# Block sums over two engines, earlier second probabilities and an earlier state load in an attention and feed-forward kernel

## The chip, the cores and the metric

The kernel runs on one core of one Trainium2 chip. The metric is the device time of one execution in microseconds (us), the median of several runs. TensorE is PE, VectorE is DVE, ScalarE is ACT, GpSimd is POOL, and SyncE, whose queue issues most transfers, is SP.

## The reference

There are 8 batches of 8 heads. Each head has 512 rows of x and 32 rows of state, both 64 wide. Rows of x attend to the state and rows of the state attend to x; the 544 rows that come out, all heads side by side, go through a feed-forward layer with a leaky relu.

```python
scores = scale * np.matmul(x, state.transpose(0, 1, 3, 2))
a = softmax(scores)                     # over the 32 rows of state
xread = np.matmul(a, state)
scores2 = scale * np.matmul(state, x.transpose(0, 1, 3, 2))
a2 = softmax(scores2)                   # over the 512 rows of x
sread = np.matmul(a2, x)
t = np.concatenate([xread, sread], axis=2)   # heads side by side: 4352 x 512
h = t @ w_in                                 # 512 x 2048
g = np.maximum(0.01 * h, h)
return g @ w_out                             # 2048 x 512
```

## The kernel before, in words

The kernel works batch by batch. The order of each engine's instructions is the order in which they are recorded in the source (a manual schedule), so an instruction that waits holds all that follow it on its engine.

**The softmax of a batch.** PE makes the scores of the batch (`a_scores`, L256) into the PSUM tile `sc`. DVE takes the maxima of blocks of 32 (`a_max`, L266, tile `mrow`), spreads them (L274) and subtracts (L280, tile `sh`): together `a_shift`. ACT takes the exponential (`a_exp`, L284, tile `e1`). DVE sums, adds a small number (L293), takes the reciprocal (L296), spreads it (L298) and multiplies (`a_probs`, L302): the first probabilities `aT`. For the second softmax, DVE takes maxima along the rows (`a_max2`, L331), ACT makes the exponentials with their sums (`a_exp2`, L337), and `a_probs2` is four DVE instructions: L345, L347 and two at L355. The second probabilities are transposed by a DMA on SP (`a_a2t`, L362; for batches 0 and 1 together `a_a2t_pair`, L369), and `a_sread` (L380) multiplies them with x.

**x and the state.** x of batch 2 and later is loaded in float32 (`load_x`, tile `xl`), cast to bfloat16 (`cast_all` on POOL, L132, tile `xb`) and transposed by a DMA on SP (`a_xt_dma`, L234, tile `xT`). The state of batches 4 to 7 is loaded by eight transfers on SP (`load_state(1)`, L203), cast on POOL (`state_cast`, L209) and transposed on SP (`state_t`, L214).

**Feed-forward.** `ff1` (L428) multiplies 128 columns of M (the state times w_in, `a_m`, copied from PSUM by `m_evict`) with `aT`, and ACT writes the leaky relu (L433) into `hT`: 16 steps a batch. The second product of batches 0 and 1 is made by plain pieces (`piece`, L533) between the steps, copied out by `y_store` (L543). The pieces of batch 0's rows 2 and 3 share one PSUM tile of two banks, `wide`. From batch 2 on, and for half of batch 1's rows, the product is done with 7 block products in place of 8. Its operands are sums of blocks of w_out, tiles `tw` 1 to 4 (`tw_sum`, L572; sum 2 needs sum 1, and sum 4 needs sum 2), and sums of blocks of h (`s_sum`, L593; for the half of batch 1 `two_sum`, L669). Batch 1's half is multiplied in the steps of batch 2 by `two_product` (L685), with additions on DVE at L695.

**Order around the change.** Before batch 1's steps: softmax of batch 1, x of batch 2, the block sums 1 and 2, pieces of batch 0, two copies of y and batch 0's second probabilities. Then batch 1's 16 steps s, with the softmax of batch 2 from s = 3 and the transpose of batch 3's x at s = 7. Then batch 2's 16 steps, with the softmax of batch 3 from s = 1.

**SP's transfers.** The transfers of SP stand in one queue, and their completions go round eight semaphores: a transfer waits for the one eight places before it.

Of the kernel before, what the change touches and what calls it, by code (L numbers as in the profile page):

```python
# [9 lines left out]
P = 128  # L10
# [5 lines left out]
NT = S // P  # L16
# [11 lines left out]
def kernel(  # L28
# [99 lines left out]
            xl[b][:, h0:h1].rearrange("p h (t d) -> p h t d", t=NT),  # L128
        )

    def cast_all(b):
        nc.gpsimd.tensor_copy(  # L132
            xt[b][:].rearrange("p t h d -> p h t d"),
            xl[b][:].rearrange("p h (t d) -> p h t d", t=NT),
        )

    def cast_x0(q, copy):
        v = q % 2
# [190 lines left out]
    def a_max2(a):  # L329
        a.m2 = att.tile([P, 2], FP32, name="mcol", tag="mcol")  # L330
        nc.vector.tensor_reduce(out=a.m2[:], in_=a.sc[:], axis=AX.X, op=ALU.max, negate=True)  # L331
# [231 lines left out]
    def tw_sum(n, j0, j1, eng):  # L563
        u, at = j0 // 4, slice(j0 % 4, j0 % 4 + j1 - j0)
        in0, in1 = {
            1: lambda: (w_block(0, 1, j0, j1), w_block(0, 0, j0, j1)),
            2: lambda: (w_block(1, 1, j0, j1), tw[1][u][:, at]),
            3: lambda: (w_block(1, 1, j0, j1), w_block(0, 1, j0, j1)),
            4: lambda: (w_block(1, 0, j0, j1), tw[2][u][:, at]),
        }[n]()  # L570
        with nc.allow_low_precision(reason="operands of bf16 products"):
            eng.tensor_tensor(out=tw[n][u][:, at], in0=in0, in1=in1, op=ALU.subtract)  # L572
# [440 lines left out]
    tw_open()  # L1013
    for j in (4, 6, 0, 2):
        tw_sum(1, j, j + 2, nc.gpsimd)
    for i in (0, 1):
        piece(0, h0, i, 1)
    open_xb(2)
# [22 lines left out]
            piece(0, h0, i, 3, copy=None, js=range(2 * v, 2 * v + 2))  # L1041
    for j in (0, 4):
        tw_sum(2, j, j + 4, nc.vector)
    for i in (2, 3):
        y_store(0, i, VEC)
    cast_all(3)
    a_probs2(a0)


# [3 lines left out]
    for s in range(16):  # L1053
        ff1(a1, h1, s)
        if s % 2:
            pb, hT, i, jq = fill[s // 2]
            piece(pb, hT, i, jq)
        if s in (1, 15):
            for u in range(2):
                tw_sum(3 if s == 1 else 4, 4 * u, 4 * (u + 1), nc.vector)  # L1060
        if s == 3:
            a_scores(a2)
            m_evict(a2, 0, a_m(a2, 0, "big"), SCA)
            a_shift(a2)
            a_max2(a2)
        elif s == 7:
            a_exp(a2)
            a_open(att_of[3], 3)
            a_xt_dma(att_of[3])
        elif s in (9, 11):  # L1070
            a_exp2(a2, s // 2 - 4)
            if s == 9:
                a_recip(a2)
                a_probs(a2)
            else:
                a_probs2(a2)
        elif s == 13:
            a_probs2(a1)
            a_a2t_pair(0)
            pm = [a_m(a2, 1, "big"), a_m(a2, 2, "sc")]  # L1080
            m_evict(a2, 1, pm[0], VEC)
            m_evict(a2, 2, pm[1], SCA)

    for b in range(2, B):
# [2 lines left out]
        a = att_of[b]  # L1089
        nxt = att_of[b + 1] if b + 1 < B else None  # L1090
        if b == 2:
            q1 = two_open(h1, 2 * P, ("S0", "S1"), "py")
            two_keep(q1, "S2")
            fill = {i: [lambda i=i: piece(1, h1, i, 3)] for i in range(2)}
            for s, n in zip((2, 3, 5, 6, 8, 9, 11), (1, 2, 6, 5, 3, 7, 4)):
                fill[s] = [lambda n=n: two_product(q1, n)]
            fill[11].append(lambda: nc.sync.dma_start(pair_rows(1, 1), q1.y[:]))
        else:
            order = (2, 6, 5, 7, 3, 4)
            fill = {  # L1100
                s: [lambda n=order[s // 2], v=s % 2: product(b - 1, n, v)] for s in range(12)
            }
            for i, n in enumerate(order):
                if n not in (2, 7):
                    fill[2 * i + 1].append(lambda n=n: after(b - 1, n))
# [3 lines left out]
        for s in range(16):  # L1109
            ff1(a, hT, s)  # L1110
            if s == 0:
                if b == 2:
                    load_x(4, nc.sync)
                if b + 2 < B:
                    open_xb(b + 2)
                if b == 7:
                    a_a2t_pair(6)
                elif b != 6:
                    a_a2t(a)
                for n in (1, 2):  # L1120
                    if b > 2:
                        s_sum(b - 1, n, 4, 8, nc.vector)
                    else:
                        two_sum(q1, n, 0, 8, nc.vector)
            elif s == 1:
                if nxt is not None:
                    a_scores(nxt)
                m_evict(a, 3, a_m(a, 3, "big"), SCA)
                if nxt is not None:
                    a_max(nxt)  # L1130
                if b > 2:
                    for j in range(0, HJ, 2):
                        s_sum(b - 1, 4, j, j + 2, nc.gpsimd)
                else:
                    for j in (0, 4):
                        two_sum(q1, 4, j, j + 4, nc.gpsimd)
                if b + 2 < B:
                    cast_all(b + 2)
            elif s == 4:
                if b == 2:  # L1140
                    load_state(1)
                    a_sread(a0)
            elif s == 7:
                if b == 2:
                    a_sread(a1)
            elif s == 13:
                if b < 6:
                    a_sread(a)
            elif s == 8:
                if b == 2:  # L1150
                    state_cast(1, nc.gpsimd)
                    state_t(1)
            elif s == 10:
                if b == 7:
                    a_sread(att_of[6])
            elif s == 12:
                if b == 7:
                    a_sread(a)
                for n in (1, 2):
                    s_sum(b, n, 0, 4, nc.vector)  # L1160
                for j in (0, 4):
                    s_sum(b, 3, j, j + 4, nc.vector)
# [25 lines left out]
            if s == 1:  # L1188
                if b > 2:
                    after(b - 1, 2)  # L1190
                if nxt is not None:
                    a_diff(nxt)
                    if b > 2:
                        a_max2(nxt)
            elif s == 3 and b == 2:
                a_max2(nxt)
                two_sum(q1, 3, 0, 8, nc.vector)
            elif s == (8 if b == 2 else 7):
                if b > 2:
                    after(b - 1, 7)  # L1200
                if nxt is not None:
                    a_probs(nxt)
                    a_probs2(nxt)
            elif s == 10 and nxt is not None:
                pm2 = a_m(nxt, 2, "phpy")
                pm0 = a_m(nxt, 0, "big")
                pm1 = a_m(nxt, 1, "sc")
                for g, copy in enumerate((SCA, VEC)):
                    copy(nxt.M[:, g, 2 * DM:3 * DM], pm2[g][:])
                m_evict(nxt, 0, pm0, VEC)  # L1210
                m_evict(nxt, 1, pm1, SCA)
# [76 lines left out]
```

## Time and profile before

| | us |
|---|---|
| median of 3 runs | 203.69 (203.34 to 203.79) |
| profiled execution | 203.5 |
| its span | 201.7 |
| PE busy | 194.7 (97%) |
| DVE busy | 160.9 (80%) |
| ACT busy | 143.8 (71%) |
| POOL busy | 62.7 (31%) |

The granted clock of TensorE is at full speed in all 40 slices of the span. A row of the timeline has the start in us, the time taken, the engine, the line of the source, the operation, out<-in with shapes, how many equal instructions were merged, and in brackets the idle time before it with what ended it. Instructions that follow each other on one engine overlap by some hundredths.

### The profile page before, as it was taken

How to read it: one execution, taken by the hardware profiler on the slowest of the kernel's cores; microseconds unless marked ns; L12 is line 12 of the kernel's file. 1: busy time of each engine (PE TensorE's matmuls, PEld its weight loads, DVE VectorE, ACT ScalarE, POOL GpSimd, SP SyncE). 2: the span in 40 equal slices, each digit the busy share in tenths (PEclk: the TensorE clock that was granted, in tenths of full speed). 3: DMA queues.
4: the chain of work that ended last, by engine and by line, in shares of the span. 5: the costliest groups of instructions: out<-in, count | busy, mean ns of one | idle time of the engine just before them, and what ended most of it. 6: DMA issues, size and time to landing. Idle time of an engine off the chain costs nothing.

```text
span 201.7 us, 4579 instructions
## 1 busy us (share of the span) xinstructions
PE 194.7 (97%) x1853; PEld 129.4 (64%) x1880; DVE 160.9 (80%) x240; ACT 143.8 (71%) x272; POOL 62.7 (31%) x67
## 2 busy tenths in 40 slices
PE   7999999999999999999999999999999999999993
PEld 2643534344476667766776677667767677799982
DVE  2766699899999999879987999699879935984712
ACT  3678676788889778777777878777958655757420
POOL 8914180030344274017500670054005500540000
PEclk9999999999999999999999999999999999999999
DMA  6999999685792798943293505220026202210115
GB/s 186 222 206 299 255 259 168 167 292 104 162 305 56 120 257 149 284 188 78 41 266 118 153 4 107 104 107 0 0 107 169 39 3 103 108 48 7 52 40 169
DMA packets 38741, 27.75 MB, mean 138 GB/s; under 512 B 24384, under 2 KB 35776, under 8 KB 38720
## 3 DMA queue, kind: packets, MB, share of 16 engines
q1 hardware_dynamic: 33552, 20.78, 39.1%
q0 software_dynamic: 4832, 6.29, 15.2%
q10 hardware_dynamic: 336, 0.39, 0.9%
q8 instruction: 14, 0.23, 0.4%
q14 instruction: 7, 0.06, 0.1%
HBM read 17.30 MB, written 8.91 MB: 130 GB/s over the span
## 4 chain that ended last, share of the span: by engine, by line
PE 78%; DVE 13%; DMA 3%; ACT 2%; issue 2%; ACTq 1%
PE ppx L628 18%; PE ph L428 17%; PE ppb L628 15%; PE ppr L685 4%; PE py L533 4%; PE pyw L533 3%; PE pf L506 3%; PE pm L407 3%; PE ppw L628 3%; PE ph L933 2%; DMA xf<-in_x_dram 2%; PE psr L380 2%; PE sc L256 1%; DVE sh L274 1%; DVE mrow L266 1%
## 5 line engine op out<-in xcount | busy, mean ns | idle before, releaser
L433 ACT ACTIVATE hT<-ph 128x512 bf16<-128x512 f32 x112 | 66.3, 603 | 26.1 <-PE ph L428 21.9
L428 PE MATMUL ph<-aT,M 128*128 128x512 bf16 x201 | 60.5, 379 | 0.1
L593 POOL TENSOR_TENSOR S<-hT,S 128x512 bf16<-128x512 bf16 x24 | 32.1, 1357 | 78.3 <-DVE S L593 61.6
L628 PEld LDWEIGHTS <-S 128*128 128x128 bf16 x384 | 37.3, 98 | 12.7
L628 PEld LDWEIGHTS <-hT 128*128 128x128 bf16 x288 | 27.6, 98 | 11.8 <-issue 1.9
L593 DVE TENSOR_TENSOR S<-hT 128x1024 bf16<-128x1024 bf16 x24 | 25.2, 1075 | 2.5 <-ACT hT L433 2.5
L428 PEld LDWEIGHTS <-M 128*128 128x128 bf16 x224 | 20.9, 98 | 9.3 <-issue 3.6
L628 PE MATMUL ppx<-tw,S 128*128 128x256 bf16 x160 | 20.7, 273 | 0.2
L533 PEld LDWEIGHTS <-hT 128*128 128x128 bf16 x96 | 9.1, 98 | 11.4 <-issue 1.3
L533 PE MATMUL py<-w_out_bf,hT 128*128 128x512 bf16 x63 | 15.9, 379 | 0.1
L132 POOL CAST xb<-xl 128x2048 bf16<-128x2048 f32 x5 | 9.8, 1969 | 15.7 <-DMA xl<-in_x_dram 15.5
L421 ACT CAST M<-pm 128x1024 bf16<-128x1024 f32 x13 | 13.2, 1014 | 0.6 <-PE pm L407 0.6
L725 DVE TENSOR_TENSOR ysb<-ppb,s 128x512 f32<-128x512 f32 x12 | 8.2, 687 | 5.5 <-PE ppb L628 5.5
L628 PE MATMUL ppb<-tw,S 128*128 128x256 bf16 x96 | 12.4, 273 | 0.2
L628 PE MATMUL ppb<-w_out_bf,hT 128*128 128x256 bf16 x96 | 12.5, 273 | 0.1
L628 PE MATMUL ppb<-w_out_bf,S 128*128 128x256 bf16 x96 | 12.3, 273 | 0.1
L628 PE MATMUL ppx<-w_out_bf,hT 128*128 128x256 bf16 x80 | 11.2, 272 | 0.2
L337 ACT ACTIVATE e<-sc,mcol 128x512 bf16<-128x512 f32 x16 | 11.0, 695 | 0.0
L628 PE MATMUL ppx<-tw,hT 128*128 128x256 bf16 x80 | 10.4, 273 | 0.2
L289 DVE TRANSPOSE_TENSOR_REDUCE r<-e 128x32 f32<-128x1024 bf16 x7 | 8.7, 1244 | 2.0 <-ACT e L284 1.9
L331 DVE TENSOR_REDUCE mcol<-sc 128x2 f32<-128x1024 f32 x8 | 9.7, 1214 | 0.0
L266 DVE TRANSPOSE_TENSOR_REDUCE mrow<-sc 128x32 f32<-128x1024 f32 x7 | 8.7, 1244 | 0.9 <-PE sc L256 0.9
(147 smaller groups left out, 310.8 us busy)
## 6 DMA issues: line engine op xcount, KB each, us to landing
out_dram<-ysb SPq DMA_DIRECT2D x11, 512.0 KB, 2.6
xl<-in_x_dram SPq DMA_DIRECT2D x5, 1024.0 KB, 6.7
out_dram<-ysb SPq DMA_DIRECT2D x9, 256.0 KB, 5.1
w_in_bf<-in_moe_w_in_dram POOLq DMA_DIRECT2D x4, 512.0 KB, 9.3
xf<-in_x_dram SPq DMA_DIRECT2D x4, 256.0 KB, 3.8
w_out_bf<-in_moe_w_out_dram POOLq DMA_DIRECT2D x4, 256.0 KB, 13.6
x<-in_x_dram POOLq DMA_DIRECT2D x2, 512.0 KB, 14.1
w_out_bf<-in_moe_w_out_dram POOLq DMA_DIRECT2D x2, 512.0 KB, 15.4
```

The costliest lines, as they stand in the source:

```text
L132: nc.gpsimd.tensor_copy(xt[b][:].rearrange("p t h d -> p h t d"), xl[b][:].rearrange("p h (t d) -> p h t d", t=NT),)
L266: nc.vector.tensor_reduce(out=m1[:], in_=flat.rearrange("p (c j) -> p c j", j=NS), axis=AX.X, op=ALU.max, apply_transpose=True,)
L289: nc.vector.tensor_reduce(out=r1[:], in_=e1[:].rearrange("p (c j) -> p c j", j=NS), axis=AX.X, op=ALU.add, apply_transpose=True,)
L331: nc.vector.tensor_reduce(out=a.m2[:], in_=a.sc[:], axis=AX.X, op=ALU.max, negate=True)
L337: nc.scalar.activation(out=a.e2[:, g], in_=a.sc[:, g, :], func=AF.Exp, bias=a.m2[:, g:g + 1], accum_out=a.r2[:, g:g + 1],)
L421: copy(a.M[:, :, cols], pm[:])
L428: nc.tensor.matmul(ph[:], lhsT=a.M[:, g, P * j:P * (j + 1)], rhs=a.aT[:, g, :], start=(g == 0), stop=(g == 1),)
L433: nc.scalar.activation(out=hT[:, j, :], in_=ph[:], func=AF.Prelu, scale=1 / SCALE, alpha=0.01)
L533: nc.tensor.matmul(y.py, lhsT=hT[:, j, P * i:P * (i + 1)], rhs=w_out_bf[:, j, :], start=(j == 0), stop=(j == 15),)
L593: eng.tensor_tensor(out=part(n), in0=in0, in1=in1, op=op)
L628: nc.tensor.matmul(q[bank][v], lhsT=lhsT, rhs=w_of(n, j), start=q["open", bank] and j == 0, stop=j == 7, skip_group_check=True,)
L725: nc.vector.tensor_tensor(out=to, in0=of, in1=in1, op=ALU.add)
```

## The change

- The two sums `tw` 3 go from DVE (batch 1's step 1, two of 128x1024) to POOL (four of 128x512: two behind the sums `tw` 1, two behind the cast of batch 3's x).
- The two sums `tw` 4 go from batch 1's step 15 to its step 1, on DVE still.
- One of the two copies of y of batch 0, ahead of batch 1's steps, goes from DVE to ACT. Both read the tile `wide`.
- Batch 1's second probabilities, and the transpose of the pair on SP behind them, go from step 13 to step 1.
- The load of the late state and its cast go from batch 2's steps 4 and 8 to batch 1's step 5, and its transpose from batch 2's step 8 to its step 0.
- Of batch 1's three sums of h on DVE, the first halves go to step 13 of batch 1, and the second halves stay.
- The cast of batch 4's x is cut in two.

PE's instructions and their order are unchanged. On SP, the transpose of the pair now stands before the last store of batch 0, the eight loads of the state behind that store, then the transpose of batch 3's x, the load of batch 4's x and the transpose of the state.

```diff
-    def cast_all(b):
-        nc.gpsimd.tensor_copy(
-            xt[b][:].rearrange("p t h d -> p h t d"),
-            xl[b][:].rearrange("p h (t d) -> p h t d", t=NT),
-        )
+    def cast_all(b, step=H):
+        for h in range(0, H, step):
+            nc.gpsimd.tensor_copy(
+                xt[b][:, :, h:h + step].rearrange("p t h d -> p h t d"),
+                xl[b][:, h:h + step].rearrange("p h (t d) -> p h t d", t=NT),
+            )
...
     for j in (4, 6, 0, 2):
         tw_sum(1, j, j + 2, nc.gpsimd)
+    for j in (0, 2):
+        tw_sum(3, j, j + 2, nc.gpsimd)
...
     for j in (0, 4):
         tw_sum(2, j, j + 4, nc.vector)
-    for i in (2, 3):
-        y_store(0, i, VEC)
+    for i, copy in ((2, SCA), (3, VEC)):
+        y_store(0, i, copy)
     cast_all(3)
+    for j in (4, 6):
+        tw_sum(3, j, j + 2, nc.gpsimd)
     a_probs2(a0)
...
-        if s in (1, 15):
-            for u in range(2):
-                tw_sum(3 if s == 1 else 4, 4 * u, 4 * (u + 1), nc.vector)
-        if s == 3:
+        if s == 1:
+            for j in (0, 4):
+                tw_sum(4, j, j + 4, nc.vector)
+            a_probs2(a1)
+            a_a2t_pair(0)
+        elif s == 3:
             a_scores(a2)
             m_evict(a2, 0, a_m(a2, 0, "big"), SCA)
             a_shift(a2)
             a_max2(a2)
+        elif s == 5:
+            load_state(1)
+            state_cast(1, nc.gpsimd)
         elif s == 7:
...
         elif s == 13:
-            a_probs2(a1)
-            a_a2t_pair(0)
             pm = [a_m(a2, 1, "big"), a_m(a2, 2, "sc")]
             m_evict(a2, 1, pm[0], VEC)
             m_evict(a2, 2, pm[1], SCA)
+            q1 = two_open(h1, 2 * P, ("S0", "S1"), "py")
+            for n in (1, 2, 3):
+                two_sum(q1, n, 0, 4, nc.vector)
...
         if b == 2:
-            q1 = two_open(h1, 2 * P, ("S0", "S1"), "py")
             two_keep(q1, "S2")
...
                 if b == 2:
                     load_x(4, nc.sync)
+                    state_t(1)
...
-                        two_sum(q1, n, 0, 8, nc.vector)
+                        two_sum(q1, n, 4, 8, nc.vector)
...
-                    cast_all(b + 2)
+                    cast_all(b + 2, 4 if b == 2 else H)
             elif s == 4:
                 if b == 2:
-                    load_state(1)
                     a_sread(a0)
...
-            elif s == 8:
-                if b == 2:
-                    state_cast(1, nc.gpsimd)
-                    state_t(1)
...
             elif s == 3 and b == 2:
                 a_max2(nxt)
-                two_sum(q1, 3, 0, 8, nc.vector)
+                two_sum(q1, 3, 4, 8, nc.vector)
```

## Prediction

> **What bounds the kernel now.** I read the page first, then the chain of work that ended last, then the timelines of DVE, ACT, PE and SP between 28 and 70 us, where every edit lies, and last the built order of both kernels with their waits.
>
> ```profile
> PE 194.7 (97%) x1853; PEld 129.4 (64%) x1880; DVE 160.9 (80%) x240; ACT 143.8 (71%) x272; POOL 62.7 (31%) x67
> ...
> PE 78%; DVE 13%; DMA 3%; ACT 2%; issue 2%; ACTq 1%
> ```
>
> TensorE is busy for 97% of the span, and the order of its instructions is the same in both kernels. So the change can be worth only what PE waits. The chain gives DVE 13%, nearly all of it in one run from 39.39 to 65.6 us. But a busy DVE costs nothing while PE has work; what counts is where PE stands. PE's timeline has two such places.
>
> ```profile
> 43.88 1.03 PE L533 MATMUL py<-w_out_bf,hT 128*128 128x512 bf16 x4
> 44.87 1.08 PE L428 MATMUL ph<-aT,M 128*128 128x512 bf16 x4
> ...
> 65.14 0.60 PE L428 MATMUL ph<-aT,M 128*128 128x512 bf16 x2
> 66.03 1.03 PE L685 MATMUL ppr<-tw,hT 128*128 128x256 bf16 x8 [0.28 <-DVE ysb L695]
> ```
>
> The chain prices four matmuls of 512 columns at 0.86 and two at 0.43. So PE was free at 65.57 and began the last of the two-row products at 66.03: 0.46 us lost (0.28 by the modelled ends), waiting for DVE's third addition at L695. At 44.74 it was free again and began ff1 step 10 at 44.87; ACT's relu of step 8 ended at 44.83 (44.24 and 0.59). There it has no room at all: what delays ACT here delays PE.
>
> ```profile
> 41.86 1.09 ACT L433 ACTIVATE hT<-ph 128x512 bf16<-128x512 f32 x2 [0.19 <-PE ph L428]
> 43.27 1.06 ACT L284 ACTIVATE e<-sh 128x1024 bf16<-128x1024 f32 x1 [0.33 <-DVE sh L280]
> 44.24 1.06 ACT L433 ACTIVATE hT<-ph 128x512 bf16<-128x512 f32 x2
> ```
>
> ACT stood idle for 0.33 until DVE gave it batch 2's shifted scores, did the exponential, and then the relus that PE wanted. From 43.27 to 48.59 ACT has no gap. DVE's work before those scores is this:
>
> ```profile
> 35.56 1.29 DVE L543 COPY ysb<-pyw 128x512 f32<-128x512 f32 x2
> 36.77 0.16 DVE L345 TENSOR_SCALAR r<-r 128x2 f32<-128x2 f32 x1
> 36.96 0.17 DVE L347 RECIPROCAL qc<-r 128x2 f32<-128x2 f32 x1
> 37.16 0.62 DVE L355 TENSOR_SCALAR a2p<-e,qc 128x512 bf16<-128x512 bf16 x2
> 37.70 1.29 DVE L572 TENSOR_TENSOR tw<-w_out_bf 128x1024 bf16<-128x1024 bf16 x2
> 39.39 1.25 DVE L266 TRANSPOSE_TENSOR_REDUCE mrow<-sc 128x32 f32<-128x1024 f32 x1 [0.41 <-PE sc L256]
> ```
>
> DVE had 0.41 to spare before batch 2's row maxima. That is the room into which step 1 is filled.
>
> **The change, part by part.** The profiled execution took 203.5 us, 201.7 of it span; the median of the three runs is 203.69, 0.19 more. I add up against 203.5 and put the 0.19 on at the end.
>
> *Step 1.* The two sums of block 3 (1.29) leave DVE and the two of block 4 (0.68 each, 1.28 by the rows at 51.12) take their place: nothing. New are batch 1's second probabilities, the same four instructions that run from 36.77 to 37.70 for batch 0: 0.93. One copy of y (L543) goes to ACT. That looks like 0.6 off DVE, but both copies read halves of one PSUM tile, and in the built order ACT's copy waits for the tile's last matmul (as DVE's first did: 35.56) and DVE's copy waits for ACT's to end. ACT's copies take 0.59, so DVE's runs from about 36.19 to 36.87, where its second one ran before (36.17 to 36.85). ACT was idle for 2.00 before 36.00, and its first relu slips by 0.1 into a gap of 0.21: free. So DVE gains nothing: 36.79 + 0.93 + 1.22 + 0.93 = 39.87 for the row maxima, against 39.39. Less a few hundredths of overlap: **0.46 late**. The exponential then starts at 43.73, the relu of step 8 ends at 45.28, and PE stands 0.46 longer. Nothing covers it: **+0.46**. All later PE times are 0.46 up.
>
> *Block 3 on POOL.* Four sums of 1.15 (4.50 for four at 25.79). Two run from 30.3 to 32.6 and two from 44.9 to 47.2, in POOL's idle times of 12.7 and 9.0. Their price is on DVE.
>
> ```profile
> 31.44 0.18 DVE L293 TENSOR_SCALAR r<-r 128x32 f32<-128x32 f32 x1
> ...
> 58.97 2.27 POOL L132 CAST xb<-xl 128x2048 bf16<-128x2048 f32 x1 [2.82 <-DMA xl<-in_x_dram]
> ...
> 60.68 0.60 DVE L293 TENSOR_SCALAR r<-r 128x32 f32<-128x32 f32 x1
> ```
>
> Beside a working POOL the small L293 took 0.60 and not 0.18. The new sums lie beside L293 of batches 1 and 2: 0.42 each. The first moves batch 1's probabilities from 34.01 to 34.43, and PE wants them at 35.15; the rest of it ends in DVE's wait for ACT's copy. The second moves batch 2's from 48.2 to 49.1 with the 0.46, and PE wants them at 51.2. Both free. (The Trainium skill, page "SBUF — State Buffer", section "Who interferes with whom", says more: an instruction holds the port pair that VectorE and GpSimd share for its whole length, and the other blocks until it ends. The row agrees: L293 ended at 61.28, POOL's cast at 61.24. By that rule the first L293 is held to about 32.6, DVE comes to its copy at 36.3, and the loss of step 1 would be 0.55 and the time about 0.1 higher.)
>
> *Step 13 and batch 2's head.* Out: the second probabilities (0.93) and block 4 (1.2). In: first halves of three sums of h; second halves follow later. No half is in the trace: between half of 0.68 and all of it; I take 0.36, as issue is a small part of such rows. Before batch 3's row maxima five halves (1.8) stand for two wholes (1.37). DVE is 1.7 lighter from 48 to 53.65, of which 0.46 and 0.42 are spent already, and the state's cast may hold it 0.4 more. So the maxima come no later than the 53.65 + 0.46 that would keep everything as it is. Earlier is worth nothing: ACT's exponential at 58.29 follows batch 0's state copies, which follow PE.
>
> *Late state and SP.* The state's cast (1.50 at 63.74) leaves the stretch where DVE makes batch 3's second probabilities; beside it L345 took 0.51 and L355 1.04, against 0.16 and 0.62. Batch 4's load is issued near 50 and not at 52.24; its cast, in two halves of about 1.0, then waits for PE's reads of batch 0 (57.68, now 58.1) and is over near 60.3, before L293 at 61.1. So L293 gets its 0.18 back too. ACT's last accumulator comes at 63.83 + 0.46 = 64.29; 0.93 and 0.41 more and the third L695 ends at 65.65, 0.4 before PE wants it (65.57 + 0.46 = 66.03). The gap closes: **-0.46**. What is late next is PE itself.
>
> The SP queue pays for it. In front of batch 3's transposed x now stand the pair's transpose (issue 2.03), a store, and eight state loads.
>
> ```profile
> 44.90 1.75 SPq L234 DMA_TRANSPOSE xT<-xb  x1
> 50.10 2.03 SPq L369 DMA_TRANSPOSE a2pT<-a2p  x1
> ...
> 57.12 5.03 SPq L203 DMA_DIRECT2D stf<-in_state_dram  x8
> ```
>
> Each SP transfer also waits for the eighth before it to land. So the seventh state load waits for the pair's transpose and the eighth for the store. The last of the four stores, issued at 39.6, took 5.9 to land, 45.5, and they land 0.6 apart: the third at 44.9. The pair's transpose took 4.6 to land, 2.6 after its issue was done: 47.0 to 47.5 behind that store. The fourth store is 0.6 behind, then the eighth load and x: issued at 47.7 to 48.4. It took 4.3 to land (others 4.9 and 5.0): 52.0 to 52.7, at worst 53.4. PE wants it at 52.58 + 0.46 = 53.04. I take no wait, with little to spare.
>
> Sum: 203.5 + 0.46 - 0.46 = 203.5, and with the 0.19, **203.7**.
>
> **The rivals.** *Faster: the delay never reaches PE.* If DVE's y copy ran beside ACT's, DVE would be 0.6 earlier, the row maxima would start at 39.39 as before, and only the closing gap were left: 203.7 - 0.46 = 203.2. For it: the halves are separate and only their tile is one. Against: the wait stands in the built order, and without it the 0.42 at L293 still eats most of DVE's gain. 0.19.
>
> *Slower: batch 3's x comes late.* SP's queue becomes the bound at PE's scores of batch 3. It decides from a landing at 53.04 on; at 53.4, or with one more slow transfer ahead (the page's transposes of a2T took 6.6 to 7.3 to land behind a 1 MB load), PE stands 0.4 to 1.0 longer: 204.1 to 204.7. For it: three waits in a row on landings, where before there was one on POOL. Against: 0.3 to 1.0 in hand. 0.22.
>
> *Slower: POOL holds DVE elsewhere.* POOL's fourth sum of h now starts between DVE's halves; a full hold of 1.15 there, one of 1.5 by the state's cast, and DVE is late again at the third L695. Three sums at L593 from 68.95 took 3.80 beside POOL, against 0.68 each. Then the gap stays: 203.7 + 0.46 = 204.2. Against: 0.4 in hand there. 0.15.
>
> *It does not do what it says.* Moving one y copy frees nothing on DVE; that is in the forecast already.
>
> **How the numbers follow.** A difference of 0.2%, 0.41 us, is about what a measurement of this kernel can tell from none. The forecast, both terms in full and nothing else, has 0.44. Faster by more than 0.41 is the first rival, 0.19; slower is the two others and a small rest, 0.38; the same is 0.43. The range goes from just under the first rival, 203.1, to 204.6, which takes in the third rival and most of the second. The likeliest case alone is 203.5 to 203.9: its two terms are read to about 0.1 each.
>
> **What would show it.** After: batch 2's row maxima (L267 there) at 39.8 to 40.0 with no idle before it; ACT's L285 at 43.7 with about 0.8 idle; ff1 step 10 at 45.3; DVE's one copy at L544 at 36.2; SP's L235 transpose of batch 3 at 47.7 to 48.4; no DVE wait before PE's last L686 product near 66.0; L294 at 0.18 near 61. I am wrong if L267 starts at 39.4, if PE waits for xT before 53, or if that product still waits for DVE.

## The result, and the profile after

The kernel after took 204.86 us (median of six runs), the kernel before 203.57 beside it: a ratio of 1.0065, 95% interval 1.0051 to 1.0079. The forecast was 203.7 with a range of 203.1 to 204.6, so the time lies above the range. One of the six executions, of 207.94 at a granted clock of 0.983, is left out of the ratio. What happened is what the second rival said: batch 3's x comes late.

The profiled execution took 204.75, its span 203.0. First the page: busy times, and the chain of work that ended last, by engine (a q marks the sequencer of an engine).

```profile
PE 196.6 (97%) x1880; PEld 129.8 (64%) x1880; DVE 161.4 (80%) x240; ACT 144.5 (71%) x273; POOL 67.3 (33%) x72
...
PE 68%; DMA 14%; DVE 6%; ACT 6%; POOL 1%; issue 1%; ACTq 1%; DVEq 0%; POOLq 0%; SPq 0%
```

PE is busy for 97% of the span, as before (the trace of before lacks 27 of the 1880 matmul records, so 194.7 and 196.6 us are not to be compared). DVE's share of the chain fell from 13% to 6%. DMA's rose from 3% to 14%, but the page gives 12 of that to loads at the start (xl 8%, w_in 4%); new behind them is 2% for xT. The chain's pieces in order of time (start, duration, what) tell the place:

```profile
40.39 1.17 DVE mrow L267
...
44.18 1.06 ACT e L285
45.77 1.08 PE ph L429 x4
49.91 4.31 DMA xT<-xb
```

DVE's run, which before went on to 65.6, ends at 44.2, and a transfer follows. PE's timeline (lines are one higher in this kernel: L533 is L534, L256 is L257, L685 is L686):

```profile
44.27 1.03 PE L534 MATMUL py<-w_out_bf,hT 128*128 128x512 bf16 x4
45.77 1.08 PE L429 MATMUL ph<-aT,M 128*128 128x512 bf16 x4 [0.48 <-ACT hT L434]
...
54.26 0.41 PE L257 MATMUL sc<-xT,st_t 64*32 64x512 bf16 x8 [0.71 <-DMA xT<-xb]
...
66.83 0.60 PE L429 MATMUL ph<-aT,M 128*128 128x512 bf16 x2
67.28 0.93 PE L686 MATMUL ppr<-tw,hT 128*128 128x256 bf16 x7
```

Two stalls are new: at ff1 step 10 (before, it began at 44.87 without one) and at batch 3's scores (52.58 before). One is gone: the last product at L686 begins 0.45 after the two ff1 matmuls ahead of it, which is their price; before it began 0.89 after them (65.14 and 66.03).

SP's timeline, a row for each run of like transfers with the time that the queue spent issuing them:

```profile
37.45 1.97 SPq L545 DMA_DIRECT2D out_dram<-ysb  x3
40.42 4.90 SPq L370 DMA_TRANSPOSE a2pT<-a2p  x1
45.41 0.53 SPq L545 DMA_DIRECT2D out_dram<-ysb  x1
45.99 3.81 SPq L204 DMA_DIRECT2D stf<-in_state_dram  x8
49.91 2.01 SPq L235 DMA_TRANSPOSE xT<-xb  x1
```

The issue of the pair's transpose, 2.03 in the kernel before, took 4.90. The fourth store and the eight loads stand behind it, and the transposed x behind them: issued at 49.91 and landed at 54.22, and PE's scores start there.

DVE and ACT, on the way to step 10:

```profile
31.86 1.07 DVE L294 TENSOR_SCALAR r<-r 128x32 f32<-128x32 f32 x1
...
36.65 0.68 DVE L544 COPY ysb<-pyw 128x512 f32<-128x512 f32 x1
...
38.18 1.28 DVE L573 TENSOR_TENSOR tw<-w_out_bf,tw 128x1024 bf16<-128x1024 bf16 x2
39.38 0.16 DVE L346 TENSOR_SCALAR r<-r 128x2 f32<-128x2 f32 x1
...
40.30 1.24 DVE L267 TRANSPOSE_TENSOR_REDUCE mrow<-sc 128x32 f32<-128x1024 f32 x1
```
```profile
42.25 1.09 ACT L434 ACTIVATE hT<-ph 128x512 bf16<-128x512 f32 x2 [0.19 <-PE ph L429]
44.18 1.06 ACT L285 ACTIVATE e<-sh 128x1024 bf16<-128x1024 f32 x1 [0.84 <-DVE sh L281]
45.14 1.07 ACT L434 ACTIVATE hT<-ph 128x512 bf16<-128x512 f32 x2
```

Batch 1's second probabilities (from 39.38) stand ahead of the row maxima, which begin at 40.30 with no idle time; ACT stands idle for 0.84 until DVE has made the shifted scores, and then PE for 0.48 until ACT has made its relu.

**One scale for all kernels.** Up to the relu that the kernel before starts at 37.77, the first of ff1 steps 2 and 3 of batch 1, the changes hardly reach PE. What the profiles differ by there comes mostly from the loads: the first block of w_in landed at 9.15 before and 9.38 after, and the kernel after stood 0.44 behind already at 21.5, where both kernels still do the same. So each kernel is compared with before relu by relu, by how far its relus in ACT's timeline stand behind. The columns say how much that grew in a stretch, in us, with the stretches in the times of the kernel before; behind 67.5 it stays as it is in all of them. Each row is one profiled execution.

| kernel | up to 37.8 | 37.8 to 44.2 | to 54.7 | to 66.2 | to 67.5 | sum behind 37.8 | ratio of times to before |
|---|---|---|---|---|---|---|---|
| after | +0.39 | +0.51 | +0.78 | +0.02 | -0.45 | +0.86 | 1.0065 |
| after, repeated | +1.43 | +0.58 | +0.72 | 0.00 | -0.44 | +0.86 | 1.0047 |
| before, repeated | -0.09 | 0.00 | 0.00 | +0.01 | +0.03 | +0.04 | 0.9985 |
| state behind x | -0.14 | +0.48 | +0.01 | 0.00 | -0.44 | +0.05 | 1.0017 |
| pair late | +0.59 | +0.45 | 0.00 | +0.01 | -0.45 | +0.01 | 1.0008 |
| pair late, probabilities behind maxima | +0.14 | 0.00 | +0.46 | +1.13 | -0.45 | +1.14 | 1.0064 |
| both copies on DVE | -0.05 | +1.17 | +0.18 | +0.01 | -0.45 | +0.91 | 1.0044 |
| sums behind cast | +0.17 | +0.45 | +0.01 | +0.01 | -0.45 | +0.02 | 1.0022 |
| whole sums | +0.14 | +0.58 | 0.00 | 0.00 | -0.45 | +0.13 | 1.0004 |
| stores on POOL | +1.83 | +0.51 | 0.00 | +0.01 | -0.45 | +0.08 | 1.0197 |
| late state alone | +0.50 | 0.00 | 0.00 | 0.00 | -0.44 | -0.44 | 1.0034 |
| late state alone, repeated | +0.29 | 0.00 | 0.00 | +0.39 | -0.16 | +0.23 | 1.0010 |
| late state and block sums | -0.11 | 0.00 | 0.00 | +0.42 | -0.29 | +0.13 | 1.0027 |
| state behind stores | +0.17 | 0.00 | 0.00 | +0.02 | -0.45 | -0.42 | 0.9983 |
| state and cast | +0.13 | 0.00 | 0.00 | +0.13 | -0.16 | -0.03 | 1.0004 |

For the kernel after: 0.39 at the start, 0.51 by the late exponential, 0.78 by the late x, 0.02 behind it, 0.45 won at the gap: 1.25, as the times of the two profiled executions say (204.75 and 203.5).

### The profile page after: what moved, and what is told of

The parts are those of the page before. It is cut to its first block, busy times and chain, and to the rows that moved or that the text cites. A ratio compares the mean times of both kernels' runs of the same rounds, so it can differ in the third digit from the quotient of the medians.

```text
span 203.0 us, 4617 instructions
## 1 busy us (share of the span) xinstructions
PE 196.6 (97%) x1880; PEld 129.8 (64%) x1880; DVE 161.4 (80%) x240; ACT 144.5 (71%) x273; POOL 67.3 (33%) x72
## 4 chain that ended last, share of the span: by engine, by line
PE 68%; DMA 14%; DVE 6%; ACT 6%; POOL 1%; issue 1%; ACTq 1%; DVEq 0%; POOLq 0%; SPq 0%
PE ph L429 20%; PE ppx L629 17%; PE ppb L629 15%; DMA xl<-in_x_dram 8%; PE ppr L686 4%; DMA w_in_bf<-in_moe_w_in_dram 4%; PE pf L507 3%; PE pm L408 3%; PE ppw L629 3%; DMA xT<-xb 2%; ACT hT L434 2%; ACT e L285 2%; PE psr L381 1%; PE py L534 1%; DVE tw L573 1%
## 5 line engine op out<-in xcount | busy, mean ns | idle before, releaser
L429 PE MATMUL ph<-aT,M 128*128 128x512 bf16 x224 | 65.3, 379 | 0.5 <-ACT hT L434 0.5
L534 PEld LDWEIGHTS <-hT 128*128 128x128 bf16 x96 | 9.0, 98 | 11.4 <-issue 1.3
L534 PE MATMUL py<-w_out_bf,hT 128*128 128x512 bf16 x64 | 16.0, 379 | 0.0
L133 POOL CAST xb<-xl 128x2048 bf16<-128x2048 f32 (+1 forms) x6 | 9.8, 1643 | 13.4 <-DMA xl<-in_x_dram 10.3
L573 POOL TENSOR_TENSOR tw<-w_out_bf 128x512 bf16<-128x512 bf16 x8 | 9.0, 1149 | 4.3 <-DMA w_out_bf<-in_moe_w_out_dram 4.3
```

The source lines that it names most:

```text
L133: nc.gpsimd.tensor_copy(xt[b][:, :, h:h + step].rearrange("p t h d -> p h t d"), xl[b][:, h:h + step].rearrange("p h (t d) -> p h t d", t=NT),
L429: nc.tensor.matmul(ph[:], lhsT=a.M[:, g, P * j:P * (j + 1)], rhs=a.aT[:, g, :], start=(g == 0), stop=(g == 1),)
L534: nc.tensor.matmul(y.py, lhsT=hT[:, j, P * i:P * (i + 1)], rhs=w_out_bf[:, j, :], start=(j == 0), stop=(j == 15),)
```

## The experiments

Each was timed in five rounds beside the kernel before; the intervals are 0.12 to 0.24% to either side (0.42% with the stores on POOL), so the traces decide where a few tenths are in question.

**State behind x.** The kernel after, with the state's loads and cast behind the transpose of batch 3's x.

```diff
-        elif s == 5:
-            load_state(1)
-            state_cast(1, nc.gpsimd)
         elif s == 7:
             ...
             a_xt_dma(att_of[3])
+            load_state(1)
+            state_cast(1, nc.gpsimd)
```

> The kernel after, with one edit: the eight loads of the late state and its cast stand behind the transpose of batch 3's x (batch 1's step 7) and not ahead of it (step 5). In the kernel after that transpose is issued at 49.9 and lands at 54.2, and PE waits for it: its lead over before grows from +0.90 to +1.68 us there. Theory SP (the nine issues ahead of x, eight of about 0.47 each, make x late): x is issued at about 46, lands near 50.3, PE makes batch 3's scores at about 53.5 without a wait, and the kernel is 0.78 faster than the kernel after, near 204.1. The state itself then lands near 54, its cast on POOL follows at about 55 and is still over before batch 3's second probabilities, so the gap of PE near 66 us stays closed. Rival A (x is late because the ring of SP is still full of the stores and of the pair's transpose, and whatever stands next is held): x is issued at 46 but lands at 53 or later, gain 0 to 0.3. Rival B (the time is lost by the delayed maxima of batch 2 and at the start, and the wait at x only shows work that would be late anyway): no change, 204.8.

Measured: ratio 1.0017 (0.9997 to 1.0037), median 203.8. SP's timeline:

```profile
39.85 5.11 SPq L370 DMA_TRANSPOSE a2pT<-a2p  x1
45.05 0.53 SPq L545 DMA_DIRECT2D out_dram<-ysb  x1
45.69 3.06 SPq L235 DMA_TRANSPOSE xT<-xb  x1
48.80 3.89 SPq L204 DMA_DIRECT2D stf<-in_state_dram  x8
```

The pair's transpose is held as long as before (5.11), but x is issued at 45.69, lands at 50.16, and PE makes the scores at 52.92 without a wait. The 0.78 is gone and no other stretch behind the start changed by more than 0.03: theory SP.

**Pair late.** The kernel after, with the pair's transpose back in step 13.

```diff
         if s == 1:
             ...
             a_probs2(a1)
-            a_a2t_pair(0)
         ...
         elif s == 13:
+            a_a2t_pair(0)
```

> The kernel after, with one edit: the transpose of the pair of second probabilities goes back to batch 1's step 13; the probabilities stay in step 1. SP then has the four stores, the eight state loads, the transpose of batch 3's x, and behind it the pair's transpose. It takes away the one issue that was held for 4.90 us. Theory SP, first form (the held issue and the eight loads are both needed to make x late): the loads are over near 46.5, x is issued by 47 and lands near 51.3, no wait, 0.78 faster than after. Second form (the loads alone suffice, because they wait for the stores to land): x is issued near 49.5 as now, lands at 54, no gain. Rival (the pair's transpose, now behind x, makes something else late: the second reads of batches 0 and 1, or batch 4's x): the 0.78 is won at x and up to 0.5 lost behind 58 us.

Measured: ratio 1.0008 (0.9993 to 1.0023), median 203.92. SP:

```profile
37.28 3.28 SPq L545 DMA_DIRECT2D out_dram<-ysb  x4
40.60 5.79 SPq L204 DMA_DIRECT2D stf<-in_state_dram  x8
46.51 1.69 SPq L235 DMA_TRANSPOSE xT<-xb  x1
48.30 2.74 SPq L370 DMA_TRANSPOSE a2pT<-a2p  x1
```

Without the held issue the loads fill the time in which the stores land, x is issued at 46.51, and there is no wait. So the late x needs both: the issue held for 4.90 and the eight loads behind it. Taking away either is enough.

**Pair late, probabilities behind maxima.** As the last one, with the second probabilities moved from ahead of batch 2's maxima to behind them.

```diff
         if s == 1:
             ...
-            a_probs2(a1)
         elif s == 3:
             ...
             a_max2(a2)
+            a_probs2(a1)
```

> The kernel after, with two edits: the transpose of the pair back in step 13, and batch 1's second probabilities (four DVE instructions, 0.93 us) in step 3 behind batch 2's maxima rather than in step 1 ahead of them. Theory of two independent losses (0.49 by the late exponential of batch 2, 0.78 by the late x of batch 3): both go, 1.27 faster than the kernel after, near 203.6, and if the 0.4 us at the start is chance, 203.2, which is before less the closed gap of 0.43. In the trace: the exponential at about 43.3 us after a short idle time, ff1 step 10 at 44.9, no wait of PE for x. Rival (the holds of DVE by POOL's block sums, 0.9 at L294 of batch 1, keep the maxima late): the exponential still starts 0.3 or more after 43.3, and the gain over the second experiment is under 0.2.

Measured: ratio 1.0064 (1.0041 to 1.0086), median 204.95: a miss. The exponential is on time (0.00 in its stretch). But behind the maxima the four instructions lie beside POOL's cast and sums of 43.0 to 47.2. DVE's timeline, then PE's:

```profile
44.37 0.58 DVE L346 TENSOR_SCALAR r<-r 128x2 f32<-128x2 f32 x1
44.98 0.17 DVE L348 RECIPROCAL qc<-r 128x2 f32<-128x2 f32 x1
45.18 2.16 DVE L356 TENSOR_SCALAR a2p<-e,qc 128x512 bf16<-128x512 bf16 x2
```
```profile
60.31 1.05 PE L686 MATMUL ppr<-tw,Sr 128*128 128x256 bf16 x8 [0.29 <-DVE ysb L696]
61.74 0.59 PE L429 MATMUL ph<-aT,M 128*128 128x512 bf16 x2 [0.39 <-ACT hT L434]
```

They took 2.9 us, not 0.93. Batch 2's probabilities came late (0.46 lost near 51.3), and then batch 3's maxima, an addition at L696 and the exponential (1.13 more). The 2 us more that DVE needed there were not to spare.

**Both copies on DVE.** The kernel after, with both copies of batch 0's y on DVE, as before.

```diff
-    for i, copy in ((2, SCA), (3, VEC)):
+    for i, copy in ((2, VEC), (3, VEC)):
```

> The kernel after, with one edit: both copies of y of batch 0 ahead of batch 1's steps are on DVE, as before. The prediction said that moving one to ACT frees nothing on DVE, because both wait for the same PSUM tile. By that, and with DVE held at L294 to 32.9 us, DVE would have made the first copy at 36.0 in the time that it now stands or makes other work: the row maxima of batch 2 move by under 0.1 and the time is the kernel after's, within 0.1. Rival (in the kernel after DVE comes to its copy at 36.65 without a wait, since the hold at L294 made it late; then the copy on ACT does free a whole copy): the maxima and the exponential of batch 2 come 0.6 later, PE's step 10 too, and the kernel is 0.3 to 0.6 slower than after.

Measured: ratio 1.0044 (1.0028 to 1.0061), median 204.53. The loss at the exponential rose from 0.51 to 1.17, which is the rival's mechanism. Its time, 0.3 to 0.6 slower than the kernel after, did not come: PE then came later to the late x and lost only 0.18 there.

**Sums behind cast.** State behind x, with all four sums of block 3 behind the cast, so that L294 of batch 1 lies beside an idle POOL.

```diff
-    for j in (0, 2):
-        tw_sum(3, j, j + 2, nc.gpsimd)
     ...
     cast_all(3)
-    for j in (4, 6):
+    for j in (0, 2, 4, 6):
         tw_sum(3, j, j + 2, nc.gpsimd)
```

> The first experiment (state behind x), with the first two of POOL's sums 3 moved behind the cast of batch 3's x, so that all four stand there and L294 of batch 1 lies beside an idle POOL. The prediction had step 1's loss as 0.46 without a hold and 0.55 with one. Theory (the prediction's wait: DVE's copy of y cannot start before ACT's has ended, near 36.2, so an earlier DVE gains little): L294 of batch 1 takes 0.18, DVE then stands before its copy, the row maxima of batch 2 come 0.1 to 0.2 earlier and the kernel is 0 to 0.2 faster than the first experiment, less what two more sums on POOL (44.6 to 49.2) hold of DVE at L294 of batch 2. Rival (DVE passes the whole hold on): the maxima come at 39.0 to 39.4, the exponential on time, 0.4 faster than the first experiment, near 203.4. Third (the longer hold behind the cast is the dearer one): batch 2's probabilities come after 51.2, PE waits for them, 0.5 or more slower.

Measured: ratio 1.0022 (1.0006 to 1.0038). DVE's timeline:

```profile
31.62 0.18 DVE L294 TENSOR_SCALAR r<-r 128x32 f32<-128x32 f32 x1
...
36.36 0.69 DVE L544 COPY ysb<-pyw 128x512 f32<-128x512 f32 x1 [0.75 <-ACT ysb L544]
```

The hold is gone, DVE comes 0.75 early to its copy and waits there for ACT's, as the prediction had it; the exponential is still 0.45 late. In the six profiles with the hold, one copy on ACT and the second probabilities in step 1 the loss is 0.45 to 0.58, so the hold costs PE at most 0.13. The second probabilities, not POOL, make step 1's loss: with them behind the maxima it was 0.00, though L294 was held there too (1.14). That the one copy on ACT frees nothing on DVE is true only where DVE arrives in time; behind the hold it saved 0.66 (1.17 less 0.51).

**Whole sums.** State behind x, with the sums of h of batch 1 whole in batch 2 again.

```diff
-            q1 = two_open(h1, 2 * P, ("S0", "S1"), "py")
-            for n in (1, 2, 3):
-                two_sum(q1, n, 0, 4, nc.vector)
...
+            q1 = two_open(h1, 2 * P, ("S0", "S1"), "py")
             two_keep(q1, "S2")
...
-                        two_sum(q1, n, 4, 8, nc.vector)
+                        two_sum(q1, n, 0, 8, nc.vector)
```

> The first experiment (the kernel after with the state behind x), with the sums of h of batch 1 whole in batch 2 again, as before, in place of first halves in step 13. The prediction took the halves as free: the row maxima of batch 3 may come 0.4 later or earlier without PE seeing it. Theory (free): no wait of PE changes, and the part from the eleventh relu to the end is the first experiment's 178.34 within 0.1. Rival (the halves, by standing beside an idle POOL, keep DVE out of POOL's way, or the other way round): ACT's exponential of batch 3 starts 0.3 or more earlier or later than in the first experiment, and PE's products at L686 wait for it: 0.3 slower.

Measured: ratio 1.0004 (0.9984 to 1.0024). Outside the stretch of the exponential, which the edit cannot reach, no stretch changed by over 0.01: the halves are free.

**Stores on POOL.** The kernel after, with the four stores of batch 0's y issued by POOL.

```diff
-        nc.sync.dma_start(rows_of(b)[i], ysb[:])
+        (nc.gpsimd if b == 0 else nc.sync).dma_start(rows_of(b)[i], ysb[:])
```

> The kernel after, with one edit: the four stores of batch 0's y are issued by POOL and not by SP. In the kernel after the issue of the pair's transpose takes 4.90 us, and in three kernels with that order it ends 0.26 us before the third store lands; in the kernel before, with the stores long gone, it took 2.03. Theory (the issue of a transpose is held on SP until the transfers queued ahead of it have drained): with the stores elsewhere the issue takes 2.0 to 3.5, the eight loads start 1.5 to 3 us earlier, x is issued at 47 to 48.5 and not 49.9, lands by 52.8, and PE waits for it 0 to 0.2: 0.6 to 0.8 faster than after, if POOL's issue costs nothing elsewhere. Rival A (the hold is the load of batch 3's x, 1 MB, issued at 36.8 and landing at 43, or the DMA engines' work whoever issues it): the issue still ends at 45, x at 54.2, no gain. Rival B (POOL's own issuing holds back its cast of batch 3's x): x late again, or later.

Measured: ratio 1.0197 (1.0156 to 1.0239), with runs from 205.69 to 208.52. The profiled one is the fastest of them and lost 1.83 of its 1.91 ahead of 37.8 us: the first block of w_in, on POOL's queue, landed at 11.56. Why the start is so late, and what the slower runs lost, is not known. Behind the start PE no longer waited for x. The issue of the pair's transpose still took 3.67, so it is not held by the queue of SP's own stores alone. With the stores on SP it ended 0.21 to 0.31 us before the third store landed in all six profiles with that order (45.32 against 45.60 in the kernel after). Here two stores were on their way, and it ended at 45.52, again 0.21 before the last of them landed (45.73). Batch 3's 1 MB load had landed 1.4 to 2.2 us before the end of the issue in all seven. So the end of the hold goes with the last store's landing, whichever queue had issued the store; why it should is not shown.

**Late state alone.** The kernel before, with only the state's loads and cast moved into batch 1, behind x (and the state's transpose into batch 2's step 0).

```diff
             a_xt_dma(att_of[3])
+            load_state(1)
+            state_cast(1, nc.gpsimd)
...
                     load_x(4, nc.sync)
+                    state_t(1)
...
-                    load_state(1)
...
-                    state_cast(1, nc.gpsimd)
-                    state_t(1)
```

> The kernel before, with one part of the change alone: the eight loads of the late state and its cast in batch 1, but behind the transpose of batch 3's x (step 7), its transpose in batch 2's step 0. Theory (the two losses belong to the early second probabilities and to what stands ahead of x on SP; the late state's cast is what made the gap of PE near 66 us): batch 2's exponential and batch 3's x come as before, the third addition at L695 no longer waits for a DVE that POOL's cast had slowed, and the kernel is 0.45 faster than before, near 203.15, a ratio of 0.9978. Rival (the gap closed in the kernel after because DVE had fewer sums of h and block sums to do, not because the cast moved): the gap stays and the time is before's within 0.1.

Measured: ratio 1.0034 (1.0015 to 1.0054). In its profile the gap closed and the sum is -0.44, as the theory had it; the times do not show it. So it was run again, with the kernels before and after.

> The late state alone once more, unchanged. Its trace showed the gap of PE near 66 us closed (0.47 less from the eleventh relu to the end than before: 177.85 against 178.32), but its time was 1.0034 of before's. Theory (a late start in those executions hid the gain; it is chance): with another start the ratio is below 1, 0.9978 at an equal start; the part behind the start is 177.85 again within 0.1. Rival (the start of this build is late each time, by 0.5 or more): the ratio is 1.002 to 1.004 again with a start of 21.0 or later.

Measured: ratio 1.0010 (0.9989 to 1.0032), and this profile is another: +0.23. SP's timeline and PE's:

```profile
46.90 4.56 SPq L203 DMA_DIRECT2D stf<-in_state_dram  x8
51.55 2.03 SPq L369 DMA_TRANSPOSE a2pT<-a2p  x1
```
```profile
57.73 0.64 PE L380 MATMUL psr<-a2pT,xb 128*128 128x64 bf16 x16 [0.23 <-DMA a2pT<-a2p]
```

As in the first profile, the loads stand ahead of the pair's transpose. It was issued 1.45 later than before and landed at 57.69 (55.80 in the first profile, 54.67 before), and PE waited; DVE's hold at L293, 1.25 against 0.60, took most of the closed gap back. The theory that only the start was late is wrong. The first series stays open: its ratio is 0.69 us, and its profile stands only 0.06 behind before in all. The other kernels timed in that series, on another chip than the rest of the experiments (sums behind cast, late state and block sums, stores on POOL), also lie above what their profiles give, by 0.26 us or more, beside the lowest median of the kernel before (203.33); in the series with the highest (203.63) all four lie below.

> The kernel before once more, unchanged. In the profiles of nine kernels the first relu of the softmax-fed steps (ACT hT, the eleventh) stands between 20.26 and 22.41 us, although all of them have the same code up to there: the first block of w_in, on POOL's queue, landed at 8.87 to 11.56. This run tells how much of that is chance from execution to execution. Theory (chance): the ratio to before is 1.000, within its interval, and the start of this profile differs from 20.54 by up to 0.6. Rival (each build has a start of its own): the start is 20.5 again and the interval excludes neither.

Before: ratio 0.9985 (0.9962 to 1.0009); its profile starts 0.09 earlier and is otherwise the same within 0.04.

> The kernel after once more, unchanged. Its profile lost 0.41 us ahead of 17 us and 0.83 behind it (0.49 at the late exponential, 0.78 at the late x, 0.43 won back at the gap). Theory (the 0.41 is chance of that execution): the part from the eleventh relu to the end is 179.15 again within 0.1, the start may be anywhere from 20.3 to 21.2, and the ratio is 1.004 to 1.006. Rival (the start is the build's): 20.97 again, ratio 1.0065.

After: ratio 1.0047 (1.0026 to 1.0068), the same 0.86 behind a start that was 1.43 late. The part behind the start is the change's; the start varies from execution to execution. Most changed kernels start a little later than the two profiles of before; whether that is more than chance is not settled.

**Late state and block sums.** The late state alone, with the block sums as in the kernel after.

```diff
+    for j in (0, 2):
+        tw_sum(3, j, j + 2, nc.gpsimd)
...
-    for i in (2, 3):
-        y_store(0, i, VEC)
+    for i, copy in ((2, SCA), (3, VEC)):
+        y_store(0, i, copy)
     cast_all(3)
+    for j in (4, 6):
+        tw_sum(3, j, j + 2, nc.gpsimd)
...
-        if s in (1, 15):
-            for u in range(2):
-                tw_sum(3 if s == 1 else 4, 4 * u, 4 * (u + 1), nc.vector)
+        if s == 1:
+            for j in (0, 4):
+                tw_sum(4, j, j + 4, nc.vector)
```

> The experiment with the late state alone, and the block sums laid out as in the kernel after (sums 3 on POOL, sums 4 in step 1, one copy of y on ACT); the second probabilities of batch 1 and the transpose of the pair stay in step 13, and the sums of h are whole. It tells what POOL's sums cost by holding DVE. Theory: in step 1 two sums of 0.68 stand for two of 0.68, and the copy that went to ACT pays for most of the 0.9 that L294 of batch 1 is held; the row maxima of batch 2 start within 0.3 of before, PE's step 10 too, and the time is that of the late state alone within 0.2. Rival (the hold of DVE at L294 of batch 2, 0.6 to 0.8, and of whatever stands beside POOL's second pair, is passed on to the maxima of batch 3 and to the third addition at L695): the gap near 66 opens again or ACT's exponential of batch 3 comes late, 0.3 to 0.6 slower.

Measured: ratio 1.0027 (1.0015 to 1.0039). The exponential of batch 2 is on time (0.00): POOL's sums cost PE nothing there. The +0.42 near 57 is the pair's transpose again (landed at 57.31). The block sums bring nothing and cost little.

**State behind stores.** The kernel before, with the loads in the idle time of SP behind batch 0's stores, and the cast on POOL behind its sums of h.

```diff
+        elif s == 5:
+            load_state(1)
         ...
                         two_sum(q1, 4, j, j + 4, nc.gpsimd)
+                    state_cast(1, nc.gpsimd)
         ...
             elif s == 4:
                 if b == 2:
-                    load_state(1)
         ...
             elif s == 8:
                 if b == 2:
-                    state_cast(1, nc.gpsimd)
                     state_t(1)
```

> The kernel before, with the eight loads of the late state in batch 1's step 5 (as in the change, where SP stands idle behind the stores of batch 0) and the cast on POOL behind its two sums of h in batch 2's step 1; all else as before, the transpose of the state in step 8 too. With the late state alone behind batch 3's x, the loads stood ahead of the pair's transpose: that landed at 57.31 and 57.69 in two of three such profiles, against 54.67 before, and PE waited 0.2 for its reads (0.38 with what it brought). Theory (any burst of nine issues costs whoever stands behind it on SP; only in the idle time behind the stores nobody wants a transfer soon): the loads end near 46.5 as in the second experiment, x of batch 3 lands near 51 (wanted at 52.6), the pair's transpose near 54.8, the cast runs near 57 beside nothing small on DVE, the gap near 66 closes in full: 0.45 faster than before, 203.1 to 203.2, ratio 0.9978. Rival (the gap closes only in part, because the cast at 57 holds DVE's sum at L669 and the rest comes late again): 0.1 to 0.3 faster.

Measured: ratio 0.9983 (0.9970 to 0.9997), median 203.34 against 203.5: shorter than before by a little more than its interval. The unchanged kernel before gave 0.9985 in another series, so the times alone would not carry this; the profile does, with 0.42 less behind the start. SP's timeline, POOL's and PE's:

```profile
40.18 5.96 SPq L203 DMA_DIRECT2D stf<-in_state_dram  x8
46.25 1.76 SPq L234 DMA_TRANSPOSE xT<-xb  x1
50.27 2.07 SPq L369 DMA_TRANSPOSE a2pT<-a2p  x1
```
```profile
56.29 1.50 POOL L209 TENSOR_SCALAR stb<-stf 128x512 bf16<-128x512 f32 x1
```
```profile
65.33 0.60 PE L428 MATMUL ph<-aT,M 128*128 128x512 bf16 x2
65.77 1.04 PE L685 MATMUL ppr<-tw,hT 128*128 128x256 bf16 x8
```

x landed at 50.54 and the pair's transpose at 54.62, both in time, and the last product at L685 follows after 0.44: the whole gap is closed. This is one profile, and the late state alone lost much of its gain when it was profiled again. Here the pair's transpose has room: PE reads at 57.22, and with the 6.18 that it took in the next experiment it would have landed at 56.45 (an estimate from these rows).

**State and cast.** The same, with the cast straight behind the loads.

```diff
         elif s == 5:
             load_state(1)
+            state_cast(1, nc.gpsimd)
         ...
                         two_sum(q1, 4, j, j + 4, nc.gpsimd)
-                    state_cast(1, nc.gpsimd)
```

> As the experiment with the state behind the stores, but with the cast on POOL straight behind the loads, where the change has it (about 48.2 to 49.8 us), beside DVE's second probabilities. Theory (the cast holds DVE's small instructions there by up to 1.5, and DVE has 0.8 to spare before batch 3's exponential): the pair's transpose is issued up to 1.5 later, lands at 56 to 56.5, just before PE's reads at 57.0, and batch 3's maxima come up to 1.2 late: 0 to 0.45 slower than the experiment with the cast at 57. Rival (the hold there is free, since batch 3's maxima have no reader before 58): the same time as that experiment, within 0.1.

Measured: ratio 1.0004 (0.9990 to 1.0018). DVE's timeline beside the cast of 48.06 to 49.71:

```profile
48.27 0.57 DVE L345 TENSOR_SCALAR r<-r 128x2 f32<-128x2 f32 x1
...
49.08 1.03 DVE L355 TENSOR_SCALAR a<-e,qc 128x512 bf16<-128x512 bf16 x2
```

0.82 of hold there sent the pair's transpose out at 51.07, 0.80 later; it landed at 57.25, 6.18 behind its issue and not 4.35, PE lost 0.13, and the gap closed by 0.16 only. In these two profiles the place of the cast is worth 0.39 us.

## Why the prediction was wrong

**SP, the step that failed.** "I take no wait, with little to spare" is wrong by 0.78. The prediction bounded the loads and x by the landings of the transfers eight places before them, and took the issue of the pair's transpose as 2.03, from a row of a time when nothing was outstanding. The queue's own issuing set the time: 4.90 for that transpose, 0.53 for the store, 3.81 for the loads. x was issued at 49.91, or 49.52 without the late start, and not at 47.7 to 48.4; its landing 4.31 later was as said. The eight loads' issue time stood in the prediction's own fence (5.03 for eight at 57.12) and was not added up. The second rival had the wait, but not its cause: it argued from "three waits in a row on landings", and each of the three landings (47.94, 48.50 and 48.68) came before the queue was free for the transfer that waits for it. Its 204.1 to 204.7 covers the sum, 203.5 + 0.51 - 0.45 + 0.78 = 204.34, with the 0.19 on top; it had 0.22 where the forecast had 0.43. The range reached up to 204.6 only for this rival. Of the 1.16 us between 203.7 and 204.86, the wait is 0.78 and step 1 and the gap 0.06. The rest, about 0.3, was in no term: the profiled execution stood 0.39 behind at the start, where no edit bears yet, but that the other executions did too is not shown.

**Step 1** was right: 0.46 forecast, 0.51 and 0.58 measured, ACT's idle time 0.84 (about 0.8). The Trainium skill's rule that was weighed there (page "SBUF — State Buffer", section "Who interferes with whom": the holder of the shared ports keeps them for its whole instruction) gave 0.55, and the trace agrees: L294 ended at 32.93 with POOL's sum at 32.90, held for 0.89 and not 0.42. What was said of the copy held only without the hold: with it DVE came to its copy at 36.65 and found no wait.

**Block 3 on POOL** was free for PE, as said, though both holds were larger (0.89 and 0.62).

**Step 13** was free, as said. A half took 0.42, not 0.36, and two were held (0.73 and 1.38).

**The late state**: -0.46 forecast, -0.45 measured, and by the cast's move, as said: the state behind stores moves that and the loads alone, and there L345 and L355 fell to 0.17 and 0.62 while L293 still took 0.68. In the kernel after L294 of batch 3 took 0.18 at 62.34. The third rival's holds came in part (0.31 and 0.96 over the 0.42 of a half), but its delay did not: L696's third addition came at 66.49 and nobody waited.

## What to carry to other kernels

Add up an issuing queue as one adds up an engine: each transfer by the time that its issue takes, and a transposing one by the longest that was seen where stores are still on their way; then see who stands behind. A burst of small loads belongs where its queue is idle and nobody behind it is wanted soon; here that place, with the cast where POOL's holds met nothing small on DVE, was the only one whose time came out below before by more than its interval. An instruction moved into another engine's way is priced by what lies beside it there: the same four took 0.93 us beside an idle POOL and 2.9 beside a busy one.

## What the runs showed of the hardware

- SP's issue of a DMA transpose (batch 3's x, the pair) took 1.69 to 2.10 in most places, 2.64 to 3.09 right behind another one (with one store between them in three kernels), 3.44 for x in the kernel with POOL's stores, and 3.67 to 5.11 for the pair's transpose issued with three stores (two in the kernel with POOL's) and batch 3's 1 MB load still on their way; there it ended 0.21 to 0.31 before the last of these stores landed.
- SP's eight state loads, back to back, took 0.42 to 0.47 of issue each in the kernel after (3.81 for all eight).
- The pair's transpose, issued at 50.0 to 51.6 ahead of batch 4's 1 MB load, took 4.35 to 4.82 to land in four profiles (state behind stores, both of before, late state alone) and 6.0 to 6.2 in three others, where it was issued at 51.07 or later. No run shows why.
- POOL's holds struck DVE's small TENSOR_SCALAR (0.18 to 1.07) and the sums of bf16 (0.68 to 1.10); the row maxima and transposes beside POOL kept their 1.24 and 1.25.
